# A fused bucketed-attention and expert-adapter kernel on one Trainium2 core: the second head's outputs and turn a slot earlier, the uniform term as a matmul in the last pairs

## The chip, the core and the metric

The kernel runs on one core of one Trainium2 chip. The core has five engines that run on their own and wait for each other through semaphores: TensorE (matmul, transposes; its weight loads are listed apart), VectorE, ScalarE (here above all exponentials), GpSimd, and SyncE, which in this kernel only issues DMA transfers. The profile calls them PE, PEld, DVE, ACT, POOL and SP. The metric is the device time of one execution in microseconds. Before the change three runs gave 185.46, 182.23 and 185.44 us (median 185.44). The profiled execution took 181.96 us; its span from the first to the last instruction is 180.2 us, and every time of a view counts from the start of that span.

## What is computed

Attention over 4 batches and 8 heads (768 rows, head dimension 64), in which a query sees only the keys of its own hash bucket of 6 sign bits; the result goes through a mixture of 8 low-rank adapters of which each row takes the best two.

```python
q_bits = (einsum('bhsd,dk->bhsk', q, proj) > 0)            # k_bits likewise
mask   = q_bucket[:, :, :, None] == k_bucket[:, :, None, :]
scores = where(mask, q @ k.T / sqrt(D), -1e9)
attn   = softmax(scores);  x = attn @ v                    # rows (b, s), columns (head, d): 3072 x 512
logits = x @ w_gate;  top 2 of 8, softmax weights w
out    = x + sum over the two of w * ((x @ A[e]) @ B[e])
```

The kernel carries the mask in the score matmul itself: next to the 64 columns of q and k stand 6 rows of signs and one constant row (the tile `aug`, 71 rows), so that a pair of rows in different buckets gets a very negative score. A query whose bucket holds no key gives the average of all v. For that a small uniform term, 2^-56 times the sums of v and a count, is added to numerator and denominator of every row.

## The kernel before

Two heads make a pair; there are 16 pairs, p = 0 to 15, four to a batch. A pair has 9 slots. In each slot TensorE computes 1024 columns of scores (`score`), and ScalarE turns them into exponentials `P`. Around that, work of neighbouring pairs is placed by hand into the slots: transposes of q and k of pair p+2 (`trans`), the hash of pair p+1, the outputs of the second head of pair p-1 and the first head of pair p (`pvmm`), their normalisation (`norm`), and the adapters ("experts") of the previous batch (`moe_slot`), in pairs 5 to 7, 9 to 11 (two tiles of 128 rows each), 13 and 14 (three). The program's order on each engine is the order in which the code emits it.

```python
def run(self):
    ...
    for p in range(N - 1):
        for s in range(9):
            self.score(p, s)
            if s == 4:
                self.moe_slot(p, s)
            if p == 0: self.first_pair(s)
            else:      self.pair(p, s)
            if s != 4:
                self.moe_slot(p, s)
    self.last_pair(N - 1, self.B - 1)

def pair(self, p, s):
    if s == 0:
        self.norm(p - 1, 0);  self.trans(p + 1, 2)
    if s == 1:
        self.pvmm(p - 1, 1, 0, 2);  self.cast(p + 1, 0);  self.cast(p + 1, 1)
    if s == 2:
        self.hash(p + 1)
    if s == 3:
        self.uniform(p);  self.pvmm(p - 1, 1, 2, 5)
    if s == 4:
        self.pvmm(p - 1, 1, 5, 6);  self.norm(p - 1, 1)
        self.trans(p + 2, 0, on_act=self.has_moe(p))
    if s == 5:
        self.vcast(p + 1);  self.trans(p + 2, 1)
        ...
    if s == 6:
        self.pvmm(p, 0, 0, 2);  self.xturn(p - 1);  self.load(p + 3)
    if s == 7:
        self.pvmm(p, 0, 2, 4)
    if s == 8:
        self.pvmm(p, 0, 4, 6)
```

`pvmm(p, h, i0, i1)` computes output tiles i0 to i1-1, six matmuls of 65 columns each, into one PSUM tile `pv` (one buffer for all pairs, so the next head's outputs wait until `norm` has read the last). `norm` adds the uniform term, divides, and writes `x`; for the second head GpSimd then casts x to `xb`, and a transposing DMA (`xturn`) turns it into `xT`, the weights of the expert logits. The load of pair p+3 (q, k and v) is queued behind that on SyncE.

```python
def uniform(self, p):                # one matmul of 130 columns, copied to SBUF by VectorE
    nc.tensor.matmul(out=ps, lhsT=self.eps, rhs=self.vb[p % 3][:, :, self.T, :], start=True, stop=True)
    nc.vector.tensor_copy(out=self.uni[p], in_=ps)

def norm(self, p, h):
    nc.vector.tensor_tensor(out=pv, in0=pv, in1=self.uni[p][:, h:h+1, :]..., op=ALU.add)   # 390 columns
    nc.vector.reciprocal(out=ri, in_=pv[:, 0:T, D])
    nc.vector.tensor_tensor(out=self.x[b][...], in0=pv[...], in1=ri..., op=ALU.mult)
    if h == 1:
        nc.gpsimd.tensor_copy(out=self.xb[b][:, hp], in_=self.x[b][...])

def hash(self, p):
    ... 4 matmuls into ps; sgn = (ps > 0) - 0.5 on VectorE
    for j in range(4):
        self.sign_dma(nc.sync, p, j, sgn)        # q and k signs of both heads into aug
```

The experts of one group: logits and low-rank product `lz` in slots 0 and 1, top two and difference `d` (`route_a`), `e = exp(d)` on ScalarE (`route_e`, slot 2), gate weights `gw` and the gated product `zm` on VectorE (`route_b`, slot 3), transposes of zm on TensorE into `ztp` and their copy `zmT` (`zmtrans`, slot 4), then from slot 6 on one tile per slot the product with B and the sum with x (`delta`: matmul `dl`, VectorE result `acc`, and after the group's last one the transfer to the output). `lz`, `ztp` and `dl` share one PSUM buffer. The last pair has a schedule of its own (`last_pair`, `third`), in which the uniform term is already a matmul, and `delta` runs partly as `tmp` on ScalarE and `acc` on GpSimd.

Of the kernel before, what the change touches and what calls it, by code (L numbers as in the profile page):

```python
# [19 lines left out]
class Emitter:  # L20


    def __init__(self, ctx, tc, q, k, v, proj, w_gate, A, Bm, out):
        self.tc, self.nc = tc, tc.nc
        nc = self.nc
        self.out = out
        B, H, S, D = q.shape
        self.B, self.H, self.S, self.D = B, H, S, D
        self.nbits = proj.shape[1]
        self.E = w_gate.shape[1]  # L30
        self.r = A.shape[2]
# [20 lines left out]
        self.xp = ctx.enter_context(tc.tile_pool(name="xp", bufs=2))  # L52
        self.smallp = ctx.enter_context(tc.tile_pool(name="smallp", bufs=4))
# [192 lines left out]
    def hash(self, p):  # L246
        if p >= self.n_pairs:
            return
        nc = self.nc
        ps = self.ps_t.tile([self.P, 384], F32, tag="t", name=f"hs{p}")  # L250
        for j in range(4):
            nc.tensor.matmul(out=ps[32 * j:32 * j + 32, :], lhsT=self.proj2,  # L252
                             rhs=self.qkT[p][:, j * 384:(j + 1) * 384], start=True, stop=True)
        sgn = self.sgp.tile([self.P, 384], BF16, tag="sgn", name=f"sgn{p}")
        nc.vector.tensor_scalar(out=sgn, in0=ps, scalar1=0.0, scalar2=0.5,  # L255
                                op0=ALU.is_gt, op1=ALU.subtract)
        for j in range(4):
            self.sign_dma(nc.sync, p, j, sgn)

    def cast(self, p, e):  # L260
        if p >= self.n_pairs:
# [51 lines left out]
    def pvmm(self, p, h, i0, i1):  # L313
        if p < 0:
            return
        if i0 == 0:
            pool, tag = (self.ps_t, "t") if (p, h) == (self.n_pairs - 2, 1) else (self.ps_v, "v")
            self.pv[p, h] = pool.tile([self.P, self.T, self.D + 1], F32, tag=tag, name=f"pv{p}_{h}")
        for i in range(i0, i1):
            self.pv_mm(self.pv[p, h][:, i, :], p, h, i, True, True)  # L320


    def uniform(self, p):
        n = self.D + 1
        ps = self.ps_t.tile([self.P, 2, n], F32, tag="t", name=f"un{p}")
        self.nc.tensor.matmul(out=ps, lhsT=self.eps, rhs=self.vb[p % 3][:, :, self.T, :], start=True, stop=True)
        self.uni[p] = self.smallp.tile([self.P, 2, n], F32, tag="uni", name=f"uni{p}")
        self.nc.vector.tensor_copy(out=self.uni[p], in_=ps)

    def norm(self, p, h):  # L330
# [4 lines left out]
        if hp == 0 and h == 0:  # L335
# [4 lines left out]
        nc.vector.tensor_tensor(out=pv[:, 0:T, :], in0=pv[:, 0:T, :],  # L340
                                in1=self.uni[p][:, h:h + 1, :].to_broadcast([P, T, D + 1]), op=ALU.add)
# [125 lines left out]
    def zmtrans(self, b, slots, last=False, far=False):  # L467
# [12 lines left out]
        self.acc[b, slots] = self.xp.tile([P, 3, self.Dm], F32, tag="acc", name=f"acc{b}_{slots[0]}")  # L480

    def delta(self, b, slots, i, last=False, by_pool=False):
        nc, P, S = self.nc, self.P, self.S
# [45 lines left out]
    def run(self):  # L529
        nc, N = self.nc, self.n_pairs  # L530
        self.prologue()
        for p in range(N - 1):
            for s in range(9):
                self.score(p, s)
                if s == 4:
                    self.moe_slot(p, s)
                if p == 0:
                    self.first_pair(s)
                else:
                    self.pair(p, s)  # L540
                if s != 4:
                    self.moe_slot(p, s)
        self.last_pair(N - 1, self.B - 1)

    def first_pair(self, s):
# [9 lines left out]
            self.cast(1, 1)  # L555
        if s == 4:
            self.hash(1)
            self.uniform(0)
        if s == 5:
            self.vcast(1)  # L560
# [10 lines left out]
    def pair(self, p, s):  # L571
# [1 line left out]
            self.norm(p - 1, 0)  # L573
            self.trans(p + 1, 2)
        if s == 1:
            self.pvmm(p - 1, 1, 0, 2)
            self.cast(p + 1, 0)
            self.cast(p + 1, 1)
        if s == 2:
            self.hash(p + 1)  # L580
        if s == 3:
            self.uniform(p)
            self.pvmm(p - 1, 1, 2, 5)
        if s == 4:
            self.pvmm(p - 1, 1, 5, 6)
            self.norm(p - 1, 1)
            self.trans(p + 2, 0, on_act=self.has_moe(p))
        if s == 5:
            self.vcast(p + 1)
            self.trans(p + 2, 1)  # L590
            if p < 4:
# [1 line left out]
                self.load_moe(2 * p - 1)  # L593
        if s == 6:
            self.pvmm(p, 0, 0, 2)
            self.xturn(p - 1)
            self.load(p + 3)
        if s == 7:
            self.pvmm(p, 0, 2, 4)
        if s == 8:  # L600
# [2 lines left out]
    def last_pair(self, p, b):  # L603
        t = [(0, 1), (2, 3), (4, 5)]
        x = self.x[b][:, :, (self.PPB - 1) * self.P:]
        for s in range(9):
# [11 lines left out]
            if s == 5:  # L618
                self.xtrans(p - 1)
                self.xtrans(p, t[0])  # L620
                self.third_x(0, x)
            if s == 6:
                self.lgz(b, t[0])
                self.route_a(b, t[0])
                self.third(1, 0)
                self.route_b(b, t[0])
            if s == 7:
                self.third(1, 1)
            if s == 8:
# [68 lines left out]
```

The softmax here doesn't subtract the row's maximum and nothing guards it: scores larger than these inputs give would overflow.

## Time and profile before

| | before |
|---|---|
| runs, us | 182.23, 185.44, 185.46 |
| profiled execution, span | 180.2 us |
| granted TensorE clock, mean | 0.982 |
| pairs 2 and 4, from first exponential to the next pair's | 8.96 us each |
| pairs 6, 7, 10, 11 (two expert tiles) | 10.05 us each |
| pairs 5 and 9 (first of a batch's experts) | 11.13 and 10.65 us |
| pairs 13, 14 (three expert tiles) | 11.09 and 11.61 us |
| last exponential ends | 167.8 us |

A line of the groups reads: line of the program, engine, operation, what is written and from what, shape, count; then busy time in all, mean ns of one, idle time of the engine before it and what ended most of that. A line of the waits reads: who waited, for whom, total us, how often, longest. A line of a timeline reads: start, length, engine, line, operation, how many were merged, and in brackets idle time just before. Ends of matmuls are modelled, so lengths of one after another overlap; the distance from start to start is what counts.

### The profile page before, as it was taken

The page shows a single profiled execution, that of the slowest core. Times are in us where ns is not written, and L with a number is a line of the kernel's source. Part 1 is how long each engine was busy: PE and PEld are TensorE (multiplying, and loading weights), DVE is VectorE, ACT ScalarE, POOL GpSimd, SP SyncE. Part 2 cuts the span into 40 slices and gives each one's busy share as a digit, 9 for nine tenths or more (in the row PEclk, how much of TensorE's full clock was granted, in tenths as well). Part 3 has the DMA queues.
Part 4 walks back from the last instruction along what each step waited for, and adds up shares of the span by engine and source line. Part 5 has one row for each costly group of instructions (what it writes and reads, how often), then busy time and mean ns, then how long its engine had stood idle before and what let it go on. Part 6 is the DMA issues. An engine that isn't in the chain of part 4 may idle for free.

```text
span 180.2 us, 5179 instructions
## 1 busy us (share of the span) xinstructions
PE 162.9 (90%) x2063; PEld 111.0 (62%) x2071; DVE 117.6 (65%) x302; ACT 153.5 (85%) x175; POOL 115.6 (64%) x140
## 2 busy tenths in 40 slices
PE   7989999999997999999999999999999989899640
PEld 6356585858585666757575675757576655587500
DVE  4653665656564787877665887878656876677751
ACT  3678999999997999999999899999998887799640
POOL 8299769898977276665667456766667356530280
PEclk9999999999999999999999999999999999999975
DMA  5935527879989359593868289695769152250044
GB/s 153 329 134 182 188 90 230 97 159 173 200 158 188 123 79 278 116 295 112 192 236 241 78 68 318 82 297 136 205 213 267 34 107 118 37 193 4 0 174 177
DMA packets 32406, 29.10 MB, mean 161 GB/s; under 512 B 17430, under 2 KB 30590, under 8 KB 32382
## 3 DMA queue, kind: packets, MB, share of 16 engines
q1 hardware_dynamic: 27420, 28.50, 56.6%
q0 software_dynamic: 4832, 0.27, 4.7%
q8 instruction: 16, 0.26, 0.7%
q14 instruction: 8, 0.07, 0.1%
q10 hardware_dynamic: 130, 0.00, 0.0%
HBM read 19.42 MB, written 6.29 MB: 143 GB/s over the span
## 4 chain that ended last, share of the span: by engine, by line
PE 65%; DVE 16%; DMA 6%; issue 3%; ACT 3%; POOL 2%; SPq 1%; DVEq 0%; ACTq 0%; POOLq 0%
PE s L302 26%; PE pv L309 13%; PE tr L232 8%; PE hs L252 6%; DMA nat<-in_k_dram 3%; PE dl L487 3%; PE lz L420 3%; DVE pv L340 2%; DVE x L345 2%; ACT P L304 2%; DVE sgn L255 2%; DVE acc L494 2%; DMA xT<-xb 2%; DVE zm L453 2%; DVE gw L451 1%
## 5 line engine op out<-in xcount | busy, mean ns | idle before, releaser
L304 ACT ACTIVATE P<-s 128x1024 bf16<-128x1024 f32 x144 | 140.8, 1026 | 12.3 <-PE s L302 9.4
L302 PE MATMUL s<-aug 71*128 71x256 bf16 (+1 forms) x396 | 86.0, 320 | 2.2 <-issue 1.1
L264 POOL CAST aug<-qkT 64x1536 bf16<-64x1536 f32 x30 | 43.9, 1464 | 15.2 <-DVE qkT L239 12.0
L309 PEld LDWEIGHTS <-P 128*128 128x128 bf16 x1080 | 43.1, 98 | 14.9 <-DVE x L345 6.6
L309 PE MATMUL pv<-vb,P 128*128 128x65 bf16 x1080 | 47.6, 194 | 1.6 <-DVE x L345 1.5
L302 PEld LDWEIGHTS <-aug 71*128 71x128 bf16 x396 | 33.9, 97 | 23.2 <-issue 11.2
L351 POOL CAST xb<-x 128x768 bf16<-128x768 f32 x15 | 12.4, 824 | 29.8 <-DVE x L345 24.2
L232 PE MATMUL tr<-ident,nat 128*128 128x128 f32 x180 | 27.8, 275 | 0.3 <-DMA nat<-in_k_dram 0.3
L239 DVE TENSOR_SCALAR qkT<-tr 128x512 f32<-128x512 f32 x38 | 25.5, 684 | 2.6 <-PE tr L232 1.3
L340 DVE TENSOR_TENSOR pv<-pv,uni 128x390 f32<-128x390 f32 x30 | 17.1, 569 | 13.5 <-PE pv L309 13.1
L232 PEld LDWEIGHTS tr<-ident,nat 128*128 128x128 f32 x180 | 20.8, 140 | 2.8 <-issue 0.6
L494 DVE SCALAR_TENSOR_TENSOR acc<-dl,rt,x 128x512 f32<-128x512 f32 x20 | 14.9, 750 | 9.3 <-PE dl L487 6.9
L255 DVE TENSOR_SCALAR sgn<-hs 128x384 bf16<-128x384 f32 x15 | 8.4, 558 | 16.0 <-PE hs L252 16.0
L345 DVE TENSOR_TENSOR x<-pv,ri 128x384 f32<-128x384 f32 x30 | 16.7, 557 | 1.0
L216 POOL TENSOR_TENSOR vs<-vn 128x384 f32<-128x384 f32 x16 | 15.9, 993 | 0.0
L214 POOL CAST vb<-vn 128x768 bf16<-128x768 f32 x16 | 13.2, 827 | 0.1
L252 PE MATMUL hs<-qkT,proj 128*32 128x384 f32 x120 | 12.8, 498 | 0.0
L420 PE MATMUL lz<-wa,xT 128*128 128x136 bf16 x96 | 9.7, 223 | 1.0 <-DMA xT<-xb 1.0
L492 POOL TENSOR_TENSOR acc<-tmp,x 128x512 f32<-128x512 f32 x4 | 5.0, 1264 | 8.0 <-ACT tmp L491 8.0
L219 POOL TENSOR_TENSOR vb<-vs,vs 128x128 bf16<-128x128 f32 x16 | 7.3, 458 | 1.3
L218 POOL TENSOR_TENSOR vs<-vs 128x128 f32<-128x128 f32 x16 | 7.3, 456 | 1.3
L420 PEld LDWEIGHTS <-xT 128*128 128x128 bf16 x96 | 6.7, 97 | 2.3 <-DMA xT<-xb 1.3
(64 smaller groups left out, 109.3 us busy)
## 6 DMA issues: line engine op xcount, KB each, us to landing
vn<-in_v_dram SPq DMA_DIRECT2D x16, 384.0 KB
nat<-in_q_dram SPq DMA_DIRECT2D x15, 384.0 KB
nat<-in_k_dram SPq DMA_DIRECT2D x15, 384.0 KB
out_dram<-acc SPq DMA_DIRECT2D x6, 512.0 KB
out_dram<-acc SPq DMA_DIRECT2D x2, 768.0 KB
out_dram<-acc SPq DMA_DIRECT2D x6, 256.0 KB
aug<-sgn SPq DMA_DIRECT2D x60, 9.0 KB
nat<-in_q_dram SPq DMA_DIRECT2D x2, 192.0 KB
```

The source lines that it names most:

```text
L216: nc.gpsimd.tensor_add(out=s3, in0=vn[:, :, 0:3, :], in1=vn[:, :, 3:6, :])
L232: nc.tensor.transpose(out=ps[:, j * P:(j + 1) * P], in_=self.nat[p][:, idx % 2, idx // 2, u * P:(u + 1) * P], identity=self.ident)
L239: nc.vector.tensor_scalar(out=out, in0=ps, scalar1=2.0 ** -5, scalar2=None, op0=ALU.mult)
L252: nc.tensor.matmul(out=ps[32 * j:32 * j + 32, :], lhsT=self.proj2, rhs=self.qkT[p][:, j * 384:(j + 1) * 384], start=True, stop=True)
L264: self.nc.gpsimd.tensor_copy(out=self.aug[p % 2][0:64, :, e * n:(e + 1) * n], in_=self.qkT[p][64 * e:64 * e + 64, :].rearrange("p (j c) -> ...
L302: nc.tensor.matmul(out=ps[:, o:o + n], lhsT=aug[0:71, 2 * h + 1, kt * P:(kt + 1) * P], rhs=q, start=True, stop=True)
L304: nc.scalar.activation(out=self.P_[p][:, s * 1024:(s + 1) * 1024], in_=ps, func=ACT.Exp, scale=128.0)
L309: self.nc.tensor.matmul(out=pv, lhsT=self.p_at(p, h, kt, i), rhs=self.vb[p % 3][:, h, self.slot(kt), :], start=(start and kt == 0), stop=( ...
L340: nc.vector.tensor_tensor(out=pv[:, 0:T, :], in0=pv[:, 0:T, :], in1=self.uni[p][:, h:h + 1, :].to_broadcast([P, T, D + 1]), op=ALU.add)
L345: nc.vector.tensor_tensor(out=self.x[b][:, :, c:c + D].rearrange("p (u e) d -> p e u d", e=2), in0=pv[:, 0:T, 0:D].rearrange("p (e u) d -> ...
L420: nc.tensor.matmul(out=lz[:, i, :], lhsT=self.xT[b][:, t, s * P:(s + 1) * P], rhs=self.wa[:, t, :], start=(t == 0), stop=(t == self.nD - 1))
L494: nc.vector.scalar_tensor_tensor(out=acc[:, i, :], in0=ps, scalar=self.rt[b, slots][:, i:i + 1], in1=self.x[b][:, slots[i], :], op0=ALU.mu ...
```

## The change

The change re-spaces the pair's slots so that the second head is finished, normalised and turned a slot sooner, and gives VectorE less to do in the last four pairs. In parts:

- Outputs of the second head as 3 + 3 tiles in slots 1 and 3, not 2 + 3 + 1 in slots 1, 3 and 4; `norm` can start at slot 4.
- `xturn` and the loads move from slot 6 to slot 5, and the four sign transfers are split: two before `xturn`, two between it and the loads.
- `zmtrans` comes after the pair's work in slot 4, and the first `delta` before it in slot 6.
- For pairs 12 to 14 (the last pair has it already) the uniform term is one matmul of 390 columns which opens the accumulation of each head's outputs; the small matmul, its copy and the addition in `norm` fall away.
- `acc` has three buffers, not two.
- In the last pair outputs go ahead of logits and routing, and the last group's intermediate transposes ahead of the second group's last delta.

```diff
-        for j in range(4):
+        self.sgn = sgn
+        for j in range(2):
             self.sign_dma(nc.sync, p, j, sgn)
+    def hash_b(self, p):
+        if p < self.n_pairs:
+            for j in range(2, 4):
+                self.sign_dma(self.nc.sync, p, j, self.sgn)
 ...  # pvmm
+            if self.uni_pe(p):
+                self.nc.tensor.matmul(
+                    out=self.pv[p, h], lhsT=self.eps, start=True, stop=False,
+                    rhs=self.vb[p % 3][:, h, self.T, :].unsqueeze(1).to_broadcast([self.P, self.T, self.D + 1]))
         for i in range(i0, i1):
-            self.pv_mm(self.pv[p, h][:, i, :], p, h, i, True, True)
+            if self.uni_pe(p):
+                self.pv_mm(self.pv[p, h][:, i, :], p, h, i, False, i == self.T - 1)
+            else:
+                self.pv_mm(self.pv[p, h][:, i, :], p, h, i, True, True)
+    def uni_pe(self, p):
+        return p >= self.n_pairs - self.PPB
 ...  # norm: the addition only where not uni_pe(p); uniform returns at once where uni_pe(p)
-        self.acc[b, slots] = self.xp.tile([P, 3, self.Dm], F32, tag="acc", ...)      # 2 buffers
+        self.acc[b, slots] = self.accp.tile([P, 3, self.Dm], F32, tag="acc", ...)    # 3 buffers
 ...  # run
-                if s == 4:
+                if s == 6:
                     self.moe_slot(p, s)
 ...
-                if s != 4:
+                if s != 6:
                     self.moe_slot(p, s)
 ...  # pair
         if s == 1:
-            self.pvmm(p - 1, 1, 0, 2)
+            self.pvmm(p - 1, 1, 0, 3)
         if s == 3:
             self.uniform(p)
-            self.pvmm(p - 1, 1, 2, 5)
+            self.pvmm(p - 1, 1, 3, 6)
         if s == 4:
-            self.pvmm(p - 1, 1, 5, 6)
             self.norm(p - 1, 1)
         if s == 5:
+            self.xturn(p - 1)
+            self.hash_b(p + 1)
+            self.load(p + 3)
             self.vcast(p + 1)
         if s == 6:
             self.pvmm(p, 0, 0, 2)
-            self.xturn(p - 1)
-            self.load(p + 3)
 ...  # last_pair
             if s == 6:
+                self.third(1, 0)
                 self.lgz(b, t[0])
-                self.route_a(b, t[0])
-                self.third(1, 0)
+                self.route_a(b, t[0], now=False)
+            if s == 7:
+                self.route_e(b, t[0])
+                self.third(1, 1)
                 self.route_b(b, t[0])
-            if s == 7:
-                self.third(1, 1)
             if s == 8:
 ...
-                self.lgz(b, t[1], far=True)
-                self.route_a(b, t[1])
         self.third(2, 1)
+        self.lgz(b, t[1], far=True)
+        self.route_a(b, t[1])
 ...
+        self.zmtrans(b, t[2], last=True, far=True)
         self.delta(b, t[1], 1, last=True, by_pool=True)
-        self.zmtrans(b, t[2], last=True, far=True)
```

More of the change, by code (lines that the diff above doesn't have):

```diff
@@ L52, in __init__ @@
         self.xp = ctx.enter_context(tc.tile_pool(name="xp", bufs=2))
+        self.accp = ctx.enter_context(tc.tile_pool(name="accp", bufs=3))
         self.smallp = ctx.enter_context(tc.tile_pool(name="smallp", bufs=4))
@@ L318, in pvmm @@
             self.pv[p, h] = pool.tile([self.P, self.T, self.D + 1], F32, tag=tag, name=f"pv{p}_{h}")
+            if self.uni_pe(p):
+                self.nc.tensor.matmul(
+                    out=self.pv[p, h], lhsT=self.eps, start=True, stop=False,
+                    rhs=self.vb[p % 3][:, h, self.T, :].unsqueeze(1).to_broadcast([self.P, self.T, self.D + 1]))
         for i in range(i0, i1):
-            self.pv_mm(self.pv[p, h][:, i, :], p, h, i, True, True)
+            if self.uni_pe(p):
[4 more added lines that the diff above has]
+        return p >= self.n_pairs - self.PPB
     def uniform(self, p):
+        if self.uni_pe(p):
+            return
         n = self.D + 1
@@ L339, in norm @@
         pv = self.pv[p, h]
-        nc.vector.tensor_tensor(out=pv[:, 0:T, :], in0=pv[:, 0:T, :],
-                                in1=self.uni[p][:, h:h + 1, :].to_broadcast([P, T, D + 1]), op=ALU.add)
+        if not self.uni_pe(p):
+            nc.vector.tensor_tensor(out=pv[:, 0:T, :], in0=pv[:, 0:T, :],
+                                    in1=self.uni[p][:, h:h + 1, :].to_broadcast([P, T, D + 1]), op=ALU.add)
         ri = self.smallp.tile([P, T], F32, tag="ri", name=f"ri{p}_{h}")
@@ L479, in zmtrans @@
             nc.vector.tensor_copy(out=self.zmT[b, slots], in_=ps)
-        self.acc[b, slots] = self.xp.tile([P, 3, self.Dm], F32, tag="acc", name=f"acc{b}_{slots[0]}")
+        self.acc[b, slots] = self.accp.tile([P, 3, self.Dm], F32, tag="acc", name=f"acc{b}_{slots[0]}")
     def delta(self, b, slots, i, last=False, by_pool=False):
@@ L557, in first_pair @@
             self.hash(1)
+            self.hash_b(1)
             self.uniform(0)
```

## The prediction, made before the changed kernel was run

> **What bounds the kernel now.** I read the page first: engine shares and costliest groups.
>
> ```profile
> span 180.2 us, 5179 instructions
> PE 162.9 (90%) x2063; PEld 111.0 (62%) x2071; DVE 117.6 (65%) x302; ACT 153.5 (85%) x175; POOL 115.6 (64%) x140
> ...
> L304 ACT ACTIVATE P<-s 128x1024 bf16<-128x1024 f32 x144 | 140.8, 1026 | 12.3 <-PE s L302 9.4
> ```
>
> Two engines are near full. ScalarE runs 144 exponentials, one per slot, which follow each other every 0.90 us when nothing holds them; TensorE is busy 90%. Next, busy time by stretch, a pair each (columns: length, then PE, PEld, DVE, ACT, POOL busy):
>
> ```profile
> 31.70:40.66 8.96, 8.80 (x123) 6.17 (x120) 5.29 (x12) 8.68 (x9) 8.05 (x10) 1.00 0.78 128
> 72.87:82.90 10.03, 9.81 (x130) 6.70 (x130) 7.83 (x22) 9.44 (x12) 6.40 (x7) 1.00 0.72 200
> 142.60:154.00 11.40, 10.40 (x133) 6.51 (x132) 8.65 (x23) 9.42 (x12) 6.40 (x7) 1.00 0.34 92
> ```
>
> A pair without the expert part lasts 8.96 us and TensorE fills it; one with two expert tiles 10.05; pairs 13 and 14, with three, 11.1 and 11.6, and there TensorE does stand. So TensorE's own work plus its short stalls sets the end, and I looked for the stalls among the waits (total us, times, longest) and in TensorE's timeline of one slot 4:
>
> ```profile
> PEld L473 <- DVE zm L453: 6.5, 9, 1.0
> PE pv L309 <- DVE x L345: 1.5, 4, 0.7
> PE tr L232 <- DMA nat<-in_k_dram: 0.3, 1, 0.3
> PE lz L420 <- DMA xT<-xb: 1.0, 1, 1.0
> ```
>
> ```profile
> 70.62 0.60 PE L302 MATMUL s<-aug 71*128 71x512 bf16 x2
> 71.34 0.28 PE L473 MATMUL ztp<-ident_bf,zm 128*128 128x128 bf16 x2
> 71.47 0.35 PE L309 MATMUL pv<-vb,P 128*128 128x65 bf16 x6
> 71.65 0.63 PE L232 MATMUL tr<-ident,nat 128*128 128x128 f32 x4
> 72.12 0.60 PE L302 MATMUL s<-aug 71*128 71x256 bf16 x3
> ```
>
> The score starts at 70.62 and takes 0.44, yet the next matmul starts at 71.34: 0.28 us lost until VectorE has made zm. From starts to starts, a score is 0.44, a group of four transposes 0.44-0.47, six output matmuls 0.18, the hash 0.78. Then the DMA queue:
>
> ```profile
> 70.28 3.17 SPq L163 DMA_DIRECT2D aug<-sgn  x4
> 74.24 1.25 SPq L391 DMA_TRANSPOSE xT<-xb  x1
> 75.54 0.86 SPq L197 DMA_DIRECT2D nat<-in_q_dram  x1
> 76.46 0.45 SPq L197 DMA_DIRECT2D nat<-in_k_dram  x1
> ```
>
> Four small sign transfers cost 3.17 us of issuing, 0.79 each. The k load lands (semaphore updates) about 3.4 us after its issue ends, and lands just in time (natN: q and k of pair N): nat6 at 50.55 for transposes that start at 50.70, nat12 at 111.50 for 111.55, nat5 at 41.99 for a fourth transpose due about 42.02, and nat11 late:
>
> ```profile
> 101.81 0.33 PE L232 MATMUL tr<-ident,nat 128*128 128x128 f32 x1 [0.28 <-DMA nat<-in_k_dram]
> ...
> 148.56 0.54 PE L309 MATMUL pv<-vb,P 128*128 128x65 bf16 x12 [0.47 <-DVE x L345]
> ```
>
> The second line is pair 14, whose outputs wait for pair 13's normalisation, itself behind the third delta.
>
> **What the Trainium skill says.** "TensorE: Matmul & The Clock Gate", section "Architectural detail: the array is 16× 32×32, not 1× 128×128", calls ScalarE's and VectorE's queues strictly first-in-first-out; the trace agrees (zmT is copied at 71.67 and the normalisation only then, 71.87), so program order is what this change moves. "DMA: Bandwidth & Descriptors", section "Issuing engines are not separate DMA queues", says the sequencer's time to start a DMA is usually small against the DMA; here it isn't: 0.72 to 0.80 us of the 1.9 us a sign transfer takes to land. "PSUM — Partial Sum Buffer", section "The four PSUM rules", says a matmul with the first flag overwrites and later ones without it add; so one wide matmul can seed all six outputs. "VectorE: DVE Perf Modes", section "Why PSUM operands drop a tier", puts float32 operands in PSUM at the plain rate; the trace's 569 ns for 390 columns fits, so removing that addition is worth its full 0.57.
>
> **The change part by part.**
> 1. *Outputs of the second head: 2+3+1 tiles become 3+3.* TensorE's sum is unchanged; 0.18 us moves from slot 4 to slot 1. Normalisation starts after slot 3's outputs: before at 32.93 in pair 2, where slot 3's outputs ended at 32.11, so about 0.6 sooner. A pair without experts gains nothing on TensorE.
> 2. *Intermediate transposes go behind the others in slot 4.* zm ends at 71.28; the transposes now fill 71.06 to 71.50, so the 0.28 stall goes. But zmT's copy now follows the normalisation: rt ends 71.56, norm 1.39, copy 0.29, so 73.28. Slot 6, with 0.6 less ahead of it less 0.18 more in slot 1, reaches the first delta, now ahead of the outputs, near 72.9: about 0.4 of new wait. Slot 7's 0.2 wait for acc goes. So about 0.3 + 0.2 gained, 0.4 lost, and what slot 1's later start hides: net 0.1 to 0.17 per pair; pairs 6, 7, 10, 11: **-0.4**.
> 3. *Transfer of x sooner.* Pair 5 waits for xT until 57.05, TensorE standing 0.97. Sooner by 0.6 plus queue room: **-0.7**.
> 4. *Uniform term on TensorE, pairs 12 to 15.* The last pair had it already. Six matmuls of 390 columns; 1024 score columns take 0.44, so 0.17 each: +1.0 in all, less three uniform matmuls (0.06 each) = +0.8. VectorE loses 6 x 0.57 and 3 x 0.29 = 4.3 us. In pairs 13 and 14 TensorE waits for VectorE: 0.55 for zm in each slot 4 (140.54 to 141.09), about 0.65 at 148.56, 0.70 at 154.86, and 0.2 before several deltas. Walked from slot 3's start in pair 13 (139.05) as zero: VectorE without the addition ends the normalisation at 2.9 and zmT at 3.3; TensorE ends slot 4 at 2.05, 5 at 2.9, 6 (score 0.44, delta 0.2, seed 0.17, outputs 0.37) at 4.1, 7 at 5.1, 8 at 6.15, where it now takes 7.25. Pair 14's slot 3 then starts at 10.35, now 11.67, and its second half ends 6.15 after that, now 7.18. That is 1.3 + 1.0 gained, less 0.35 more in pair 13's slot 1 (three outputs and a seed): 22.7 us for both becomes about 20.7 if nothing else holds them. I keep **-1.5**, as the loads bite here (term 5). Pair 12 keeps its matmul: **+0.3**.
> 5. *Two sign transfers go behind the x transfer, ahead of the loads.* The x transfer leaves sooner by 0.6 (no experts) or 0.2-0.3, but 2 x 0.79 = 1.6 us stand before the loads, so these leave about 1.0 later, less the 0.3-1.3 by which the q issue already lingers in some pairs (0.86 above against 0.57). The loop from slot 4 to the next slot 4 is: norm start 0.2, norm 1.4, cast 0.95, transfer 1.3, signs 1.6, q and k 1.1, landing 3.4 = 9.95, against a fourth transpose at 0.77: a pair without experts needs 9.2, not 8.96; with experts about 10.0. Pairs 3, 8, 12 lose 0.2-0.3 each, pair 9 (a 6.17 us landing already) 0.5: **+1.2**.
> 6. *Third acc buffer.* No wait for an output transfer shows in front of acc: 0.
> 7. *Last pair.* The outputs go ahead of the expert logits, so the 1.68 us between two exponentials shrinks by about 0.25. Afterwards e of tiles 2-3 (now at 169.22) waits for logits that come after all outputs (its input near 169.85) and holds ScalarE's tmp and xT copy by about 0.6; zmT of the last tiles moves ahead of a 0.68 tmp; but the fourth output's issue then holds the last two in the queue by about 0.5. **+0.4**.
>
> Sum: -0.4 -0.7 -1.5 +0.3 +1.2 +0.4 = **-0.7 us**. I could not fix terms 4 and 5 to better than about 1 us each.
>
> **The rivals.** *The loads become the bound:* for it, landings within 0.1 to 0.5 us of their use in half the pairs; against it, some q issues already linger longer than the rest, so signs may fill a gap. All pairs at 9.2 or 10.1: +2 to +3 us, 184.5 from the low level, 188 from the high one. *TensorE's stalls go and the loads don't bite:* zm waits in nine places, two normalisation stalls, one xT stall; then -3 to -4 us, 178.5 to 182. *ScalarE takes over:* nine exponentials at 0.9, the copy of one transposed group 0.5 and e 0.2 make 8.8 per expert pair, below TensorE's own sum of 9.4 (10.05 less the 0.6 of stalls), and 8.1 against 8.8 in the others; so it becomes the bound in single slots and of no pair: no change to the sum.
>
> **Range and chances.** The times before lie at two levels, 182.23 and about 185.45, and the profiled run took 181.96; -0.7 gives 181.5 or 184.7. I take 183.2, between. The range adds the rivals: 179.6 to 186.4. Over 2% needs some 3.7 us, which only the second rival reaches: 0.22. Slower by over 2% needs the loads to bind everywhere: 0.11. Rest 0.67.
>
> **What would show it.** Right: no wait of TensorE for zm in expert pairs with two tiles, a new one before the first delta; xT's wait in pair 5 mostly gone; SyncE issuing two signs, transfer, two signs, loads; waits of the transposes for nat growing from 0.8 us in all to 2-4; pairs 13 and 14 down by 1 to 2 us together; the stretch after the last exponential not shorter. Wrong: nat waits unchanged (term 5 invented, faster), nat waits over 5 us (slower), or a tail shorter by 1 us.

## The result, and the profile after

The changed kernel took 184.01, 184.24, 184.45 and 193.01 us, the kernel before, beside it on the same chip, 182.23 to 185.46 us. The ratio is 1.012, with a 95% interval of 1.008 to 1.017: about 2 us slower, less than 2%, where the prediction had 0.7 us faster. (Executions that lie over 1.5% above the fastest of the same kernel are left out of ratios here; where too few remain, only the single times are given.)

First the page of the changed kernel: span, busy times of the engines, the chain that ended last (by engine, then by line), and the group of the exponentials; behind it the chain of the kernel before.

```profile
span 182.2 us, 5178 instructions
PE 162.6 (89%) x2073; PEld 111.3 (61%) x2074; DVE 112.5 (62%) x293; ACT 153.2 (84%) x175; POOL 115.3 (63%) x140
...
PE 53%; DMA 21%; DVE 7%; SPq 6%; ACT 4%; issue 3%; POOL 2%; DVEq 0%; ACTq 0%; POOLq 0%
PE s L309 22%; DMA nat<-in_k_dram 14%; PE pv L316 11%; PE tr L233 7%; DMA aug<-sgn 4%; PE hs L253 4%; SPq L164 3%; ACT P L311 3%; PE dl L508 2%; SPq L198 2%; DMA xT<-xb 2%; PE lz L441 2%; DVE pv L361 1%; DVE x L366 1%; PE warm L184 1%
...
L311 ACT ACTIVATE P<-s 128x1024 bf16<-128x1024 f32 x144 | 141.0, 1027 | 15.5 <-PE s L309 14.3
```

```profile
PE 65%; DVE 16%; DMA 6%; issue 3%; ACT 3%; POOL 2%; SPq 1%; DVEq 0%; ACTq 0%; POOLq 0%
```

TensorE's busy time is the same (162.6 against 162.9) and VectorE has 5.1 us less, so there is no new work. But the exponentials now wait 14.3 us for scores instead of 9.4, and in the chain DMA rose from 6% to 21%: of those, 14% are the loads of k (3% before). Where it happens shows by pairs. Lengths in us, from a pair's first exponential to the next pair's, read from ScalarE's timeline; "tail" runs from the end of the last exponential to the end of the span; e1 and e9 are experiments told below.

| pair | 2 | 3 | 4 | 5 | 6 | 7 | 8 | 9 | 10 | 11 | 12 | 13 | 14 | 15 | tail |
|---|---|---|---|---|---|---|---|---|---|---|---|---|---|---|---|
| before | 8.96 | 9.01 | 8.96 | 11.13 | 10.05 | 10.05 | 9.16 | 10.65 | 10.05 | 10.05 | 9.17 | 11.09 | 11.61 | 9.18 | 12.42 |
| after | 9.29 | **11.13** | 8.88 | 10.89 | 10.37 | 10.16 | 9.37 | 9.85 | 9.84 | **11.16** | 8.83 | 11.08 | 10.34 | **10.01** | 12.95 |
| e1 | 8.92 | 8.96 | 8.95 | 10.87 | 10.14 | 9.88 | 9.01 | 11.74 | 9.85 | 9.85 | 9.11 | 10.39 | 10.34 | 9.41 | 12.98 |
| e9 | 8.91 | 9.38 | 9.37 | 9.91 | 9.85 | 9.85 | 8.97 | 9.90 | 9.84 | 9.85 | 9.02 | 10.33 | 10.34 | 9.34 | 12.24 |

Three places carry most of the loss: pair 3 (+2.1), pair 11 (+1.1), pair 15 with the tail (+1.4); pairs 2, 6, 7 and 8 add 1.0 together. Pairs 9, 10 and 14 gained 2.3 together. (The first exponential began 0.5 us earlier in the changed kernel's trace, at 8.37; in the fourteen traces of this case it begins between 8.23 and 9.06, whatever was changed. From there on the trace lost 2.5 us.) The stretches of pairs 2, 3, 10 and 14 of the changed kernel (length; PE, PEld, DVE, ACT, POOL busy with counts; granted clock, DMA share, GB/s):

```profile
28.07:37.36 9.29, 8.94 (x120) 6.11 (x118) 5.45 (x11) 8.68 (x9) 8.51 (x11) 1.00 0.86 158
37.36:48.49 11.13, 9.13 (x120) 6.03 (x118) 5.50 (x12) 8.68 (x9) 9.18 (x11) 1.00 0.83 147
108.02:117.86 9.84, 9.75 (x132) 6.86 (x130) 7.55 (x22) 9.40 (x11) 6.38 (x8) 1.00 0.81 198
148.94:159.28 10.34, 9.97 (x133) 6.25 (x131) 6.68 (x21) 9.07 (x10) 6.38 (x7) 1.00 0.42 95
```

Pairs 2 and 3 do the same work, but in pair 3 TensorE stands for 2.0 of 11.13 us. Pair 10 shows what the re-spacing was for: 9.84 us, with TensorE busy 9.75 of them; in pair 14 it is 9.97 of 10.34. What TensorE waits for (total us, times, longest):

```profile
PEld tr L233 <- DMA nat<-in_k_dram: 4.9, 8, 1.0
PE tr L233 <- DMA nat<-in_k_dram: 2.9, 6, 0.7
PEld L494 <- DVE zm L474: 2.6, 3, 1.0
PE s L309 <- DMA aug<-sgn: 1.4, 2, 0.9
PE tr L233 <- DVE x L366: 1.1, 1, 1.1
```

The wait for zm fell from 9 times to 3. In its place stand eight waits of the transposes' weight loads for the load of k, where there was one (0.5 us), and two scores that wait for signs, which before had none. The matmuls' row for k shows for the most part the same standing time as the weight loads' row, so 2.9 us is nearer to what TensorE lost there than the 7.8 of both. TensorE's timeline of the slot of pair 6 that the prediction showed of the kernel before:

```profile
72.27 0.60 PE L309 MATMUL s<-aug 71*128 71x512 bf16 x2
72.71 0.49 PE L233 MATMUL tr<-ident,nat 128*128 128x128 f32 x3
73.86 0.33 PE L233 MATMUL tr<-ident,nat 128*128 128x128 f32 x1 [0.66 <-DMA nat<-in_k_dram]
```

The transposes now follow the score at once, and the gap that zm made is gone; but the fourth transpose, the first that needs k, comes 1.15 us after the first of the three for q. The same slot in pair 3, where the most was lost:

```profile
42.60 0.52 PE L233 MATMUL tr<-ident,nat 128*128 128x128 f32 x3 [1.07 <-DVE x L366]
43.84 0.33 PE L233 MATMUL tr<-ident,nat 128*128 128x128 f32 x1 [0.72 <-DMA nat<-in_k_dram]
```

The first wait is put down to VectorE's x, but it was for q: the semaphore of q's load was complete at 42.46, and in pair 10 the same transposes start before x does (112.45 against 113.70). So TensorE stood 1.8 us for the two loads that had been queued in pair 2. SyncE's queue there (start, length):

```profile
31.30 1.53 SPq L164 DMA_DIRECT2D aug<-sgn  x2
34.22 2.00 SPq L412 DMA_TRANSPOSE xT<-xb  x1
36.32 1.52 SPq L164 DMA_DIRECT2D aug<-sgn  x2
37.90 0.43 SPq L198 DMA_DIRECT2D nat<-in_q_dram  x1
38.38 0.46 SPq L198 DMA_DIRECT2D nat<-in_k_dram  x1
```

The order is the intended one, but the first two signs were issued until 32.83, the queue then does nothing until 34.22, and after the transfer it spends 1.52 us on signs before the loads can leave. By the semaphores' updates q landed at 42.46 and k at 43.79.

### The profile page after: what moved, and what is told of

Its sections match the earlier page's. It is cut to its first block, busy times and chain, and to the rows that moved or that the text cites. A ratio compares the mean times of both kernels' runs of the same rounds, so it can differ in the third digit from the quotient of the medians.

```text
span 182.2 us, 5178 instructions
## 1 busy us (share of the span) xinstructions
PE 162.6 (89%) x2073; PEld 111.3 (61%) x2074; DVE 112.5 (62%) x293; ACT 153.2 (84%) x175; POOL 115.3 (63%) x140
## 4 chain that ended last, share of the span: by engine, by line
PE 53%; DMA 21%; DVE 7%; SPq 6%; ACT 4%; issue 3%; POOL 2%; DVEq 0%; ACTq 0%; POOLq 0%
PE s L309 22%; DMA nat<-in_k_dram 14%; PE pv L316 11%; PE tr L233 7%; DMA aug<-sgn 4%; PE hs L253 4%; SPq L164 3%; ACT P L311 3%; PE dl L508 2%; SPq L198 2%; DMA xT<-xb 2%; PE lz L441 2%; DVE pv L361 1%; DVE x L366 1%; PE warm L184 1%
## 5 line engine op out<-in xcount | busy, mean ns | idle before, releaser
L311 ACT ACTIVATE P<-s 128x1024 bf16<-128x1024 f32 x144 | 141.0, 1027 | 15.5 <-PE s L309 14.3
L271 POOL CAST aug<-qkT 64x1536 bf16<-64x1536 f32 x30 | 43.8, 1461 | 20.7 <-DVE qkT L240 17.9
L316 PEld LDWEIGHTS <-P 128*128 128x128 bf16 x1080 | 42.1, 98 | 11.6 <-DVE x L366 3.3
L309 PEld LDWEIGHTS <-aug 71*128 71x128 bf16 x396 | 33.0, 97 | 23.4 <-issue 11.2
L316 PE MATMUL pv<-vb,P 128*128 128x65 bf16 x1080 | 45.2, 193 | 0.2
L233 PE MATMUL tr<-ident,nat 128*128 128x128 f32 x180 | 29.1, 276 | 4.1 <-DMA nat<-in_k_dram 2.9
L233 PEld LDWEIGHTS tr<-ident,nat 128*128 128x128 f32 x180 | 21.8, 140 | 11.4 <-DMA nat<-in_k_dram 4.9
L361 DVE TENSOR_TENSOR pv<-pv,uni 128x390 f32<-128x390 f32 x24 | 13.6, 567 | 11.3 <-PE pv L316 10.8
L441 PE MATMUL lz<-wa,xT 128*128 128x136 bf16 x96 | 9.1, 223 | 1.6 <-DMA xT<-xb 0.9
L508 PE MATMUL dl<-Bcat,zmT 128*128 128x512 bf16 x23 | 9.2, 399 | 0.8 <-ACT zmT L498 0.7
L364 DVE RECIPROCAL ri<-pv 128x6 f32<-128x6 f32 x30 | 5.8, 193 | 3.9 <-PE pv L316 3.1
```

The lines of the kernel that those rows point to most:

```text
L233: nc.tensor.transpose(out=ps[:, j * P:(j + 1) * P], in_=self.nat[p][:, idx % 2, idx // 2, u * P:(u + 1) * P], identity=self.ident)
L271: self.nc.gpsimd.tensor_copy(out=self.aug[p % 2][0:64, :, e * n:(e + 1) * n], in_=self.qkT[p][64 * e:64 * e + 64, :].rearrange("p (j c) -> ...
L309: nc.tensor.matmul(out=ps[:, o:o + n], lhsT=aug[0:71, 2 * h + 1, kt * P:(kt + 1) * P], rhs=q, start=True, stop=True)
L311: nc.scalar.activation(out=self.P_[p][:, s * 1024:(s + 1) * 1024], in_=ps, func=ACT.Exp, scale=128.0)
L316: self.nc.tensor.matmul(out=pv, lhsT=self.p_at(p, h, kt, i), rhs=self.vb[p % 3][:, h, self.slot(kt), :], start=(start and kt == 0), stop=( ...
```

## The experiments

**Theory A** (the prediction's first rival, with term 5): the two sign transfers in front of the loads make q and k late. **Theory B**: the change's own work costs, that is the wide matmuls of the uniform term and the last pair's new order (e4 tests the last pair alone). **Theory C**, from e9 on: what is left is the wait for the transposing transfer xT, whose landing varies.

### e1: all four signs ahead of the transfer of x, the rest as in the changed kernel

```diff
-        for j in range(2):
+        for j in range(4):
             self.sign_dma(nc.sync, p, j, sgn)
     def hash_b(self, p):
-        if p < self.n_pairs: ...   # signs 2 and 3 behind xturn
+        return
```

> The changed kernel with all four sign transfers issued ahead of the x transfer again, everything else as changed. Theory A (two signs between the x transfer and the loads make q and k land too late, and make the late signs late themselves): about 2 us come back, 181.5 to 182.5 us; the waits of the transposes for nat fall from 2.9 us to under 1, pair 3 from 11.1 to about 9.3, pair 15's first slot from 1.70 to about 0.95. Theory B (the loss is in the wide seed matmuls and in the last pair's new order): 183.8 to 184.5, nat waits may fall but the time does not.

Measured: 180.27 us in the profiled execution, 184.01, 184.19 and 184.74 in the others. SyncE's queue in pair 2 of e1, which starts within 0.03 us of where it starts in the changed kernel:

```profile
31.33 3.14 SPq L164 DMA_DIRECT2D aug<-sgn  x4
34.57 1.76 SPq L410 DMA_TRANSPOSE xT<-xb  x1
36.38 0.58 SPq L198 DMA_DIRECT2D nat<-in_q_dram  x1
37.01 0.46 SPq L198 DMA_DIRECT2D nat<-in_k_dram  x1
```

With two signs ahead of it the transfer of x left at 34.22, with four at 34.57; the load of q left at 37.90 and 36.38, that of k at 38.38 and 37.01. The split therefore brought the transfer of x 0.35 us and cost the loads 1.4 to 1.5. They landed 2.45 us later than in e1 (42.46 and 43.79 against 40.01 and 41.33); the other 1.0 is the spread of landings. In pairs 6, 7, 10 and 11 the transfer of x leaves 7.22 to 7.25 us after the pair's first exponential in both kernels, so there the split brought nothing. The reason is in SyncE's own waits, of the changed kernel and then of the kernel before:

```profile
SPq L412 <- POOL xb L372: 19.4, 13, 1.9
```

```profile
SPq L391 <- POOL xb L351: 4.0, 9, 0.7
```

What holds the transfer of x is GpSimd's cast to `xb`. Before, the queue used that time to issue signs. In e1 one wait for k is left, 0.7 us on the weight load and 0.4 on the matmul; by the table pairs 2, 3, 6, 7, 8 and 13 together are 4.1 us shorter than after, pair 11 is 1.3 and pair 15 is 0.6 shorter. In the trace that is A, against B. But the profiled execution lost 1.9 us in pair 9, where TensorE waits for xT:

```profile
97.07 0.23 PE L439 MATMUL lz<-wa,xT 128*128 128x136 bf16 x1 [1.72 <-DMA xT<-xb]
```

And the three untraced executions were no shorter than the changed kernel's, which is the time that B forecast. Whether xT did that too, e10 asks. Whether the split helps xT is open: in the four traces with the split on SyncE's queue (after, e2, e3, e4) no first slot of pairs 9 and 13 waits for xT, while in the five with all four signs first and the transposing DMA (e1, e5, e6, e11, e12) four of ten transfers landed 4.4 to 4.6 us after their issue instead of 2.8.

### e2: loads before the signs, in slot 1

```diff
         if s == 1: ...
+            self.load(p + 3)
         if s == 5: ...
-            self.load(p + 3)
```

> The changed kernel with the load of pair p+3 issued in slot 1, ahead of the signs and the x transfer, whose order stays split. Theory A: nat waits vanish, 180.5 to 182 us, better than with the signs put back. A rival within A (the transfers queue behind 1.2 MB of loads): signs and xT land 2 to 4 us later, TensorE waits for aug at the pair's start instead, and the time is 183 or more. Theory B: about 184.

Measured: median 187.14 us, ratio 1.026 (1.018 to 1.034), the slowest variant of the changed order: the rival within A. k is hardly waited for any more (one wait of 0.2 us), but TensorE's waits now read:

```profile
PE s L309 <- DMA aug<-sgn: 4.9, 4, 2.3
```

The signs stand behind the loads, in the queue and on the DMA engines. The first head's signs issued in pairs 1 and 3 landed 4.9 to 7 us after their issue, and TensorE stood 2.31 and 1.84 us for them; at the end of these waits the granted clock fell to 0.50, for 3.41 and 6.83 us (the last section has more of this). Pairs 1 to 4 grew to 11.63, 10.28, 11.01 and 11.47 us; there the adapters' weights are transferred as well. Pair 15 took 0.8 more than in e1. From pair 6 on each two-tile pair took 9.85. So who stands behind whom is late, in both directions, and the early load does no visible harm from pair 6 on; e5 uses it from pair 5 on. The Trainium skill ("DMA: Bandwidth & Descriptors", section "Queues, rings and completion order") says that each DMA engine takes the descriptors of a ring in order; the late landing of 9 KB of signs behind 1.2 MB of loads agrees with that.

### e3: the kernel before with the signs split

```diff
-        for j in range(4):
+        for j in range(2):
             self.sign_dma(nc.sync, p, j, sgn)
         if s == 6: self.xturn(p - 1)
+            self.hash_b(p + 1)       # signs 2 and 3
             self.load(p + 3)
```

> The kernel before with one part of the change alone: two of the four signs go behind the x transfer and ahead of the loads. Theory A: slower by 1 to 2.5 us (183.3 to 184.8 against 182.25), with nat waits of 2 us or more. Theory B: no difference, within 0.3 us.

Measured: 188.79, 192.22, 194.73 and 196.28 us, no ratio; even the shortest is 6.5 us over the median of before (182.3), far above what was expected. The waits of the longest execution, which is the profiled one:

```profile
PEld tr L232 <- DMA nat<-in_k_dram: 6.4, 7, 1.8
PE tr L232 <- DMA nat<-in_k_dram: 4.7, 6, 1.5
PE s L308 <- DMA aug<-sgn: 2.0, 1, 2.0
```

The split alone, in the old spacing, makes the kernel slower, and waits for k come with it, so B is not needed for a loss. Not all of the loss is waiting: pairs 12 and 15 lost 5.4 and 4.9 us against before, where TensorE stood 2.3 for q and k and 2.0 for signs, and after each of these the granted clock was 0.50 for 6.83 us. Why the changed kernel pays less for the split is not shown; it queues x and the loads a slot sooner.

### e4: the changed kernel with the old last pair

> The changed kernel with the last pair's order of before. My tail term (new order costs): 0.3 to 0.8 us faster than the changed kernel, about 183.6; from the last exponential to the end 12.4 us instead of 12.95. Rival (the new order gains in the slots before the last exponential as much as it costs after): no difference, 184.2.

The edit is the last hunk of the change's diff, reversed. Measured: median 184.46 us, ratio 1.013 (1.005 to 1.020), the same as the changed kernel; the expected gain did not show in the time. The tail is 12.40 instead of 12.95, but pair 4 took 12.23 in this execution, after waits of 0.58 for q and 0.89 for k and 3.41 us at a granted clock of 0.50. The new last pair costs about half a microsecond in the trace; the experiment could not size it by its time.

### e5: all four signs first, early loads from pair 5 on, the old last pair

```diff
# e1 and e4, and:
         if s == 1: ...
+            if p >= 5: self.load(p + 3)
         if s == 5: ...
-            self.load(p + 3)
+            if p < 5: self.load(p + 3)
```

> The changed kernel with three things put right: all four signs ahead of the x transfer, the loads from pair 5 on in slot 1 ahead of the signs (before pair 5 behind the x transfer, where the adapters' weights share the queues), and the last pair's order of before. Theory A says the schedule of the change is a gain once the transfers are out of its way: pairs 6, 7, 10, 11 at 9.85, pairs 13 and 14 at 10.4 each, span near 176, 177 to 179 us. Theory B (the change's own work costs): 181 or more.

Measured: median 178.14 us, ratio 0.979 (0.973 to 0.985). With the signs back, the loads early and the last pair as before, the kernel is 2.1% faster than before; of that the early loads may be 0.4% (e8). What remained in the profiled execution (the longest, 180.73) are above all two waits for xT at the first matmul of a batch's experts, of 1.48 and 1.52 us in pairs 9 and 13; pair 13's in TensorE's timeline:

```profile
137.18 0.23 PE L439 MATMUL lz<-wa,xT 128*128 128x136 bf16 x1 [1.52 <-DMA xT<-xb]
```

### e6: e5 without the seed matmul

`uni_pe` returns False, so VectorE adds the uniform term in pairs 12 to 14 again.

> The same, with the uniform term of pairs 12 to 14 back on VectorE. My term 4 says the matmul form is worth 1.5 us or a little more in pairs 13 and 14 and costs 0.3 in pair 12: 1 to 2 us slower than the kernel with it, 178.5 to 180.5. Rival (pairs 13 and 14 gain from the re-spaced outputs and deltas, not from the seed): within 0.4 us of it.

Measured: median 179.13 us (178.47 to 182.40), ratio 0.983 (0.977 to 0.989), about 1 us over e5. Pairs 13 and 14 take 10.68 + 11.37 = 22.05 us, against 10.33 + 10.34 = 20.67 with the seed (e9, the same there but for xT). So the seed is worth 1.4 of the 2.0 us between before (22.70) and e9, and the re-spacing 0.65. Pair 12 is 9.02 with (e9) and without.

### e7: the changed kernel, the two late signs on GpSimd's queue

```diff
-            self.hash_b(p + 1)
             self.load(p + 3)
+            self.hash_b(p + 1)       # in it: nc.sync becomes nc.gpsimd
```

> The changed kernel with the two late sign transfers issued by GpSimd's queue, so that nothing stands between the x transfer and the loads on SyncE. Theory A, in the form that the issuing time of SyncE is what delays the loads: nat waits under 1 us, 182 us or less. In the form that the transfers themselves clog the queues: nat waits as in the changed kernel, 184. Pair 15's first slot stays long (1.5 or more) either way.

Measured: 178.74 to 185.27 us, median 181.98, no ratio. No wait of a pair's transposes for k is left in the trace, though the same bytes move, and in pair 2 the two signs still leave (35.35) ahead of the loads (36.73): this points to the issuing time on SyncE's queue and not to the sign transfers' traffic. But xT came later (waits of the profiled, longest execution):

```profile
PE lz L441 <- DMA xT<-xb: 5.9, 3, 2.5
```

In pair 4 the transfer left 1.7 us later after the pair's first exponential than in the changed kernel, as GpSimd, which casts `xb`, now also issues; in pairs 8 and 12 it left within 0.15 us of the same place but landed 4.4 and 5.7 us after its issue instead of 2.8.

### e8: the kernel before with early loads from pair 5 on

> The kernel before with its loads in slot 1 from pair 5 on and nothing else. If the loads were nearly hidden before, as its nat waits of 0.3 to 0.8 us say: 0.3 to 1.0 us faster, 181.3 to 182. If the loads bound the kernel already before the change: 2 us or more.

The edit is that of e5's `load`, in slot 1 and slot 6. Measured: median 181.52 us, ratio 0.996 (0.993 to 0.999). In the kernel before, the loads were very nearly hidden; moving them is worth 0.4% there.

### e9: e5, with the turn that the experts wait for on TensorE

```diff
         if s == 5:
-            self.xturn(p - 1)
+            if p % self.PPB:
+                self.xturn(p - 1)
         if s == 7: ...
+            if p % self.PPB == 0:
+                self.xtrans(p - 1)    # six transposes on TensorE, one copy on VectorE
```

> The repaired kernel (signs first, loads in slot 1 from pair 5 on, old last pair), with the turn of x that ends a batch (in pairs 4, 8 and 12) done by six TensorE transposes and a VectorE copy in slot 7 instead of by the transposing DMA. Theory C (what is left of the loss, and most of the spread from run to run, is TensorE waiting for xT at the start of pairs 5, 9 and 13, which took 1.0 to 2.9 us in these profiles): those first slots fall to about 1.05, at a cost of 0.3 us in each of three pairs; 176 to 177.3 us, spread under 1 us. If the wait only moves (copy, logits): no gain, 178.

Measured: median 177.04 us (176.61 to 177.79), ratio 0.976 (0.973 to 0.980): the shortest of all, below both kernels. Its page, the k waits, and the added transposes in TensorE's timeline:

```profile
span 175.3 us, 5224 instructions
PE 162.2 (93%) x2092; PEld 112.1 (64%) x2092; DVE 113.4 (65%) x296; ACT 152.1 (87%) x175; POOL 115.5 (66%) x140
```

```profile
PEld tr L233 <- DMA nat<-in_k_dram: 1.1, 2, 0.6
```

```profile
53.98 0.50 PE L422 MATMUL xtp<-ident_bf,xb 128*128 128x128 bf16 x6
```

0.33 us of TensorE (to the next start, 54.31), three times, replaces a transfer whose landing varied from 2.8 to 4.6 us after its issue (5.7 in e7). Slot 0 of pairs 5, 9 and 13 takes 0.99 us in each; in the kernel before they took 2.19, 1.21 and 1.19. And the six executions lie within 1.2 us.

### e10: e1 with the same turn

> The changed kernel with all four signs first and the turn at a batch's end on TensorE; loads behind the x transfer and the new last pair, as in the change. Theory A with C: the kernel with the signs first was held at 184 in most runs by its xT waits; without them 179 to 180.5, some 4 us under the changed kernel. If signs first alone does little: 182 or more.

Measured: median 178.38 us (177.39 to 178.53), ratio 0.982 (0.977 to 0.987). e1, from which it differs in these three turns alone, had 184 in three of four executions, at a mean granted clock of 0.952 to 0.967, where its profiled one and all four of e10 have 0.978 to 0.981. So what held e1 there hung on these turns; long waits for xT with falls of the clock after them would do it, but no trace of a 184 was taken. Even here TensorE waits 0.9 us for k in pair 3 (10.03 us), with the signs first. What is missing is the changed kernel with its split and these turns on TensorE: without it the cost of the split is sized in the traces and by e3, and not in the times of the changed kernel itself.

### e11: e5 with the old place of the experts' work in slots 4 and 6

```diff
-                if s == 6:
+                if s == 4:
                     self.moe_slot(p, s)      # ahead of the pair's work
```

> The repaired kernel with the experts' work in its old place: intermediate transposes ahead of the pair's work in slot 4, first delta after it in slot 6. My term 2 says pairs 6, 7, 10, 11 become longer by 0.1 to 0.2 us each, 9.95 to 10.05 against 9.85, and the waits for zm return (6.5 us on the weight loads against 1.6). Rival (zm is waited for less anyway, as slot 3 is fuller): 9.85 to 9.9.

One execution, 180.28 us. Pairs 6, 7, 10 and 11 take 10.11, 10.11, 10.10 and 10.11 us, against 9.85 each in e5, and the stall for zm is back (1.6 us, twice, in e5):

```profile
PEld L492 <- DVE zm L472: 6.0, 9, 1.0
```

### e12: e5 with two `acc` buffers

> The repaired kernel with two acc buffers instead of three. My term 6 says no difference in any pair; in the last stretch the third group's acc may wait for the first group's transfer to the output, 0.1 to 0.3 us. Rival (the third buffer is what keeps VectorE from standing behind 6 us output transfers): 0.5 us or more in the expert pairs.

One execution, 181.72 us. The only wait of `acc` for an output transfer (2.0 us on VectorE, once) lies in the tail, which is 12.05 us with two buffers and with three. The longer time comes from waits for xT (pair 9, 13.16 us, with a fall of the clock) and for k (pair 4, 9.98), where no `acc` waits for an output.

## Why the prediction was wrong in direction and right in range

The range held, and so did the likeliest outcome, within 2% (0.67). That says little: the range is 6.8 us wide, and its middle, 183.2, was put between the two levels of before; from the lower one -0.7 gives 181.5, and 184.3 came. The sum had the wrong sign: -0.7 forecast, about +2 measured. Most of the change's parts did what was said of them or better; **term 5 failed in size**, and part of its reasoning was wrong.

**Terms 1 and 2, outputs 3+3 and the order of the experts' work: right, and too small.** The gap before the intermediate transposes went. With the loads out of the way the four two-tile pairs took 9.85 us each where there were 10.05: 0.20 per pair, not 0.10 to 0.17, and 0.8 us instead of 0.4. The order of the experts' work alone is worth 0.26 per pair (e11). The step that was mis-sized is the new wait ahead of the first delta. It was put at 0.4; the trace of e9 has six such waits (the weight load on VectorE's zmT) of at most 0.3 us, 1.9 in all, and pair 10's TensorE is busy for 9.74 of 9.84 us. A pair without experts gained nothing, as said: 8.92 in e1, 8.96 before.

**Term 3, the transfer of x sooner: wrong.** Slot 0 of pair 5 went from 2.19 to 2.09 us, not down by 0.7; slots 0 of pairs 9 and 13 gained 0.3 together. In pair 4 the transfer left 0.5 us sooner after the pair's first exponential (6.11 against 6.64), but landed 4.12 us after its issue instead of 3.77. The transfer's issue is held by GpSimd's cast, and its landing varies by more than what was to be gained. That these waits change between traces with the same code around them (pair 13 waits in e5 and not in e12, which differs from it in the `acc` buffers alone) was not seen from one trace of before. They may also be why before's times lay at two levels; that is an inference, as there is no trace of a long execution of before.

**Term 4, the seed: right.** -1.5 was kept for pairs 13 and 14; the seed alone gave -1.4, and with the re-spacing both pairs go from 22.70 to 20.67, the figure walked in the prediction ("about 20.7 if nothing else holds them"). In the changed kernel itself pair 13 lost 0.7 of it to k. The +0.3 for pair 12 did not come (9.02 either way, 8.83 in the changed kernel); instead slot 0 of pair 15 took 1.10 in e5, 0.93 in e6.

**Term 5, two signs ahead of the loads: right in sign and mechanism, too small by a factor of three to five.** 1.2 us was forecast. Pairs 2, 3, 6, 7, 8 and 13 lost 4.1 against e1, and the waits for k add up to 7.8 us over both rows, counted as the prediction counted its 0.8, where it called over 5 the sign of "slower". Two steps failed. First, the delay was laid on a loop with landings of 3.4 us, and each pair lost only what the loop exceeds its length by. For pairs 2 and 8 that was near (9.29 and 9.37, where 9.2 was said). But landings spread: in pair 3 k's took 4.95 us from the end of its issue, and there alone 2.2 us went. The trace of before had it already: 3.2 to 4.2 us in eleven of the thirteen loads of k behind the start, and 5.2 and 5.7 in two.

Second, the term looked only at who needs k, not at who needs the signs. The signs of pair 12's first head left SyncE from 121.53 on; the loads, held up by the split, had left from 118.16 on and an output transfer at 120.28, 3.4 and 1.3 us ahead of them, where in the kernel before it was 4.8 and 2.3. One sign transfer landed only at 128.24, 5.9 us after its issue (at most 4.0 before), and pair 11 ended 1.3 late. Pair 15 needs the second head's signs in its second slot; these were now issued until 158.96, and the pair lost 0.6. The two scores that waited:

```profile
128.33 0.59 PE L309 MATMUL s<-aug 71*128 71x512 bf16 x3 [0.92 <-DMA aug<-sgn]
160.55 0.39 PE L309 MATMUL s<-aug 71*128 71x256 bf16 x2 [0.43 <-DMA aug<-sgn]
```

In the places where it hurt, the split costs 6.0 us in this trace (4.1 + 1.3 + 0.6). The balance closes: e1's span against before's is -1.7 (178.5 against 180.2, with 1.9 for xT in pair 9 in it), the split +6.0, and pair 9 without that wait -1.9, pair 12 and the rest -0.4; that is +2.0. Whether the 1.9 belongs to the split or to chance is open (e1); if it does, the split costs 3.7 in all, the difference of the two spans.

**Term 6, the third buffer: right.** Nothing before, nothing in e12.

**Term 7, the last pair: right in sign.** The tail is 12.49 to 13.35 us in the five traces with the new order (e1, e2, e7, e10 and the changed kernel's 12.95), and 12.05 to 12.42 in the nine with the old. The means are 12.87 and 12.19, so +0.7, close to the +0.6 of the later part. The -0.25 between two exponentials did not come: 1.65 and 1.03 us where there were 1.68 and 0.92.

**The rivals.** "The loads become the bound" was put at +2 to +3 us with every pair at 9.2 or 10.1, and 0.11 for slower by 2%. Its size came true, about +2, but not its pattern: a few pairs stood for one or two microseconds and others not at all. "The stalls go and the loads don't bite" is what e5 made of the change by another order in one queue and the old last pair, and e9 with three turns moved to TensorE as well: 178.1 and 177.0 us, the -3 to -4 and a little more. ScalarE took over no pair: in pair 14 of e9 it is busy 9.07 of 10.34 us, TensorE 9.97.

What stays open: what makes the landing of xT vary between executions. No experiment was made on it; e9 only stopped depending on it.

## What to carry to other kernels

On a queue that issues in order, look at what each entry waits for before moving another one behind it: here two small transfers ahead of a transfer that waits anyway cost it 0.35 us or nothing, and behind it they cost the loads 1.4 to 1.5. Ask too who reads what was moved: the signs had readers of their own. Where a stretch of DMA has only tenths of a microsecond to spare, count with the longest landings in the trace and not with the typical one: in pair 3 a landing 1 us longer than in e1 came on top of 1.4 us of later issue, and 2.2 us went. A re-spacing that disappoints need not be undone: with the signs back and three transfers replaced (e10) the rest was worth 1.8%.

## What the runs showed of the hardware that was not expected

After some waits the granted TensorE clock fell for a few microseconds. In e12, TensorE waited 1.58 us for xT until 97.95; in e5, 1.52 us until 137.18. The stretches about these waits, first of e12, then of e5 (columns as above):

```profile
95.00:98.41 3.41, 1.67 (x14) 1.19 (x14) 1.92 (x4) 1.85 (x2) 2.08 (x3) 1.00 0.90 152
98.41:101.82 3.41, 3.41 (x34) 1.95 (x32) 0.42 (x3) 1.81 (x2) 1.61 (x2) 0.50 0.68 238
101.82:105.23 3.41, 3.41 (x42) 2.55 (x39) 2.82 (x10) 2.79 (x6) 0.00 (x0) 1.00 0.02 5
```

```profile
132.45:135.86 3.41, 3.04 (x47) 2.24 (x42) 1.22 (x4) 3.38 (x4) 2.53 (x4) 1.00 0.34 67
135.86:139.27 3.41, 2.09 (x33) 1.59 (x33) 0.54 (x4) 1.32 (x2) 2.92 (x2) 1.00 0.01 1
139.27:142.69 3.42, 3.42 (x43) 2.20 (x43) 2.57 (x12) 2.99 (x4) 0.00 (x0) 1.00 0.01 3
```

In e12 the clock is 0.50 from 98.41 to 101.82 and then 1.00 again, and two of the slots in it took 2.30 and 1.74 us where 0.9 to 1.1 is usual, so this wait of 1.58 us was followed by about two more lost. After e5's wait of nearly the same length it stays at 1.00, so the length of one wait does not decide it.

The clock records of the fourteen traces show what goes with it. Between the start and the tail there are seven falls, each to 0.50, four of 3.41 us (e2, e4, e7, e12) and three of 6.83 (e2 and twice in e3), and within one trace all falls begin whole multiples of 3.41 us apart: in e2 at 30.40 and 50.88, six times 3.41. So lay each trace out in stretches of 3.41 us, placed so that a fall begins where a stretch does; the fall that every trace has in its tail, where TensorE has little to do, gives the place in the others. Then every fall follows a stretch in which TensorE was busy for at most 0.57 of the time (from 9 us on, 21 falls), and none follows one with 0.58 or more at full clock (over 650 stretches); at 0.57 both happened. In e12 the wait fell into one stretch, 1.67 of 3.41 us busy (0.49); in e5 two stretches shared it, 0.89 and 0.61 busy. This is a pattern of these traces and was not tested by an experiment of its own. It means that two waits of a microsecond close together, as in pair 4 of e4, can cost more than they last.
